# Placing the tiles that DMA writes at multiples of 512 bytes in SBUF, in a two-block cached-attention decode kernel

## The chip, the cores and the metric

The kernel runs on one core of a Trainium2 chip (trn2). The metric is the device time of one execution in microseconds. All runs used here are fast, that is, none was slowed by a lower clock (the granted clock of the tensor engine was 0.72 to 0.74 in every run). In what follows, HBM is the memory that holds the inputs, and SBUF the memory of the core, in 128 partitions, into which DMA (the copying engines) brings them.

## The reference

Two independent attention blocks, A and B, each decode one token for two batch entries; their outputs are concatenated. Cut to what matters:

```python
def _A_ref(x, k_cache, v_cache, wq, wo):      # B is the same
    B, Sq, D = x.shape                        # 2, 1, 640
    Hq, Dh = 32, 192                          # K and V: [2, 32, 8192, 192] bf16
    q = (x @ wq).reshape(B, Sq, Hq, Dh).transpose(0, 2, 1, 3)
    scores = einsum("bhqd,bhkd->bhqk", q, k) * (Dh ** -0.5)
    o = einsum("bhqk,bhkd->bhqd", softmax(scores), v)
    return o.transpose(0, 2, 1, 3).reshape(B, Sq, Hq * Dh) @ wo
```

Each K and V element is used once. The kernel has to bring 837 MB from HBM into SBUF, of which K and V are 805 MB. wq and wo are 15.7 MB each.

## The kernel before

A unit `u` is one (block, head, batch entry); there are 128. The sync engine issues the loads, with two buffers each for K and V. The vector engine multiplies K by q and reduces, the scalar engine sums a quarter of the rows and does the exponentials, the tensor engine multiplies V by the probabilities. What the change and the argument touch:

```python
sb = lambda name, shape, dt: es.enter_context(nc.sbuf_tensor(name, shape, dt))
...
kb = [sb(f"kb{i}", [128, T, Dh], BF16) for i in range(NK)]      # T = 64 rows: 24576 bytes per partition
vb = [sb(f"vb{i}", [128, T, Dh], BF16) for i in range(NV)]
prodA = [sb(f"prodA{i}", [128, NA_MAX, Dh], BF16) for i in range(2)]
# ... cut: the other tiles of the engines
wqs = sb("wqs", [128, 2, DC, HG * Dh], BF16)                    # 1536-byte pieces
wos = sb("wos", [128, HG, 3, D], BF16)                          # four slots of 3840 bytes
# ... cut

def sp_wo(w):
    # ... cut
    src = blocks[blk]["wo"][h0 * Dh:(h0 + HG) * Dh, :].rearrange("(pr p i) n -> p pr (i n)", p=128, i=3)
    return dma(wos[:, (w % 2) * HG // 2:(w % 2 + 1) * HG // 2, :, :].rearrange("p pr i n -> p pr (i n)"), src, wosem)

def sp_k(u, part=None):
    blk, h, b, g = unit(u)
    src = blocks[blk]["k"][b, h].rearrange("(p t) d -> p t d", p=128)
    if part is None:
        return dma(kb[u % NK][:], src, ksem[u % NK])
    # ... cut: the first K load comes in two parts

def sp_v(u, t0=0, t1=None, sm=None):
    # ... cut: the last four V loads come in pieces
        return dma(v_tile(u)[:], src, vsem[u % NV])
```

The kernel's instruction streams are emitted with loops (eight units per turn) on the vector and scalar engine and four on the tensor engine; this matters below for how the experiments are built.

Of the kernel before, what the change touches and what calls it, by code (L numbers as in the profile page):

```python
# [8 lines left out]
BF16 = mybir.dt.bfloat16  # L9
# [93 lines left out]
def build_kernel(nc, blocks, out, cfg=None):  # L103
    cfg = dict(cfg or {})
    NBLK = len(blocks)
    B, Hn, Sk, Dh = blocks[0]["k"].shape
    D = blocks[0]["x"].shape[2]
    assert B == 2 and Dh == 192 and Sk % 256 == 0 and D % 128 == 0
    T = Sk // 128
    DC = D // 128  # L110
# [10 lines left out]
    NK = cfg.get("NK", 2)  # L121
    NV = cfg.get("NV", 2)
    HG = cfg.get("HG", 4)
    if Hn % HG != 0:
        HG = 2
# [20 lines left out]
        return 4 * (qg // 2) + (qg % 2)  # L146

    with ExitStack() as es:
        sb = lambda name, shape, dt: es.enter_context(nc.sbuf_tensor(name, shape, dt))
        ps = lambda name, shape, dt: es.enter_context(nc.psum_tensor(name, shape, dt))  # L150
        sem = lambda name: es.enter_context(nc.semaphore(name))

        kb = [sb(f"kb{i}", [128, T, Dh], BF16) for i in range(NK)]
        vb = [sb(f"vb{i}", [128, T, Dh], BF16) for i in range(NV)]
        prodA = [sb(f"prodA{i}", [128, NA_MAX, Dh], BF16) for i in range(2)]
        prodD = sb("prodD", [128, ND_MAX, Dh], BF16)
        sc = [sb(f"sc{i}", [128, T], F32) for i in range(2)]
# [3 lines left out]
        pb = [sb(f"pb{i}", [128, T // 2, 33], BF16) for i in range(NPB)]  # L161
        rs = [sb(f"rs{i}", [128, 1], F32) for i in range(2)]
        qbc = [sb(f"qbc{i}", [128, 2, Dh], BF16) for i in range(4)]
        wqs = sb("wqs", [128, 2, DC, HG * Dh], BF16)
        wos = sb("wos", [128, HG, 3, D], BF16)
        xT = [[sb(f"xT{k}_{b}", [128, DC], BF16) for b in range(B)] for k in range(NBLK)]
        xbc = [[sb(f"xbc{k}_{b}", [128, DC, 128], BF16) for b in range(B)] for k in range(NBLK)]
        o_sb = sb("o_sb", [33, 2, 2, Dh], F32)
# [290 lines left out]
        for u in range(NU):  # L459
            g = u // B  # L460
# [154 lines left out]
def bass_concat_heads__gqa_block_cached__mha_block_cached__decode_kernel(  # L615
    nc: bass.Bass,
    A_x: bass.AP,
    A_k_cache: bass.AP,
    A_v_cache: bass.AP,
    A_wq: bass.AP,  # L620
    A_wo: bass.AP,
    B_x: bass.AP,
    B_k_cache: bass.AP,
    B_v_cache: bass.AP,
    B_wq: bass.AP,
    B_wo: bass.AP,
    out: bass.AP,
):
    blocks = [
        dict(x=A_x, k=A_k_cache, v=A_v_cache, wq=A_wq, wo=A_wo),  # L630
        dict(x=B_x, k=B_k_cache, v=B_v_cache, wq=B_wq, wo=B_wo),
    ]
    build_kernel(nc, blocks, out)
# [28 lines left out]
```

## Time and profile before

| | before |
|---|---|
| time, median of 4 runs | 1975.26 us (1974.32 to 1975.52) |
| bytes over DMA | 836.79 MB on the load queue |
| busy share: load queue (16 engines) / vector / tensor / scalar | 99.6% / 84% / 56% / 46% |

Lines of the page of the kernel before: busy time of each engine; GB/s in 40 equal slices of the span; packets; the load queue with its packets, MB and share of the 16 DMA engines; and the chain of waits that ended last, by engine.

```profile
PE 1111.1 (56%) x5004; PEld 589.3 (30%) x5004; DVE 1655.7 (84%) x962; ACT 904.1 (46%) x4743; POOL 151.5 (8%) x270
...
GB/s 384 425 429 427 430 426 431 430 425 430 428 430 430 426 431 427 430 430 426 430 426 430 429 427 431 428 427 428 430 431 428 429 428 430 430 426 430 431 429 290
DMA packets 56476, 837.12 MB, mean 424 GB/s; under 512 B 7416, under 2 KB 18304, under 8 KB 23680
...
q1 hardware_dynamic: 56432, 836.79, 99.6%
...
DMA 72%; PE 22%; DVE 5%; issue 1%; SPq 0%; ACT 0%; DVEq 0%
```

The reader should see that nothing but the loads sets the pace: the queue is hardly ever idle (99.6%), its rate is flat from the second slice to the last but one (425 to 431 GB/s), and the chain is mostly loads (72%). The table of windows of the kernel before says the same for three stretches (columns: the stretch and its length, busy time and count of each engine, granted clock, DMA share, GB/s):

```profile
200.00:800.00 600.00, 333.75 (x1507) 177.09 (x1506) 513.67 (x298) 281.71 (x1480) 44.49 (x80) 0.72 1.01 429
800.00:1400.00 600.00, 345.41 (x1546) 182.90 (x1545) 507.84 (x298) 275.88 (x1447) 29.36 (x80) 0.72 1.01 429
1400.00:1900.00 500.00, 284.54 (x1279) 151.12 (x1277) 426.38 (x247) 232.28 (x1219) 23.82 (x65) 0.72 1.01 429
```

Below the page, the trace has one record per DMA packet, with start, duration and size. A packet here is one contiguous row. Here is a digest of the kernel before (durations in ns; smaller pieces of the first and last loads are left out):

```
row (bytes)  what     packets   shortest  median  mean
24576        K, V     32128     912       916     916.7
3840         wo        4096     149       152     152.9
1536         wq        9600      65        68      68.6
```

That is 2008 K/V packets, 256 of wo and 600 of wq for each of the 16 engines, practically without gaps (99.6% of the span). Among the pieces left out are 512 of 12288 bytes; the shortest of them took 460 ns. So two rows of 12288 bytes take at least 920 ns and one of 24576 at least 912: as an estimate from these two, each packet has 8 ns that do not grow with its size (149 and 65 ns, set against 912 in the same way, give 7.7 and 8.5). The records do not name the engine: which packet follows which on one engine is inferred from their ends and starts.

### The profile page before, as it was taken

How to read it: one execution, taken by the hardware profiler on the slowest of the kernel's cores; microseconds unless marked ns; L12 is line 12 of the kernel's file. 1: busy time of each engine (PE TensorE's matmuls, PEld its weight loads, DVE VectorE, ACT ScalarE, POOL GpSimd, SP SyncE). 2: the span in 40 equal slices, each digit the busy share in tenths (PEclk: the TensorE clock that was granted, in tenths of full speed). 3: DMA queues.
4: the chain of work that ended last, by engine and by line, in shares of the span. 5: the costliest groups of instructions: out<-in, count | busy, mean ns of one | idle time of the engine just before them, and what ended most of it. 6: DMA issues, size and time to landing. Idle time of an engine off the chain costs nothing.

```text
span 1973.5 us, 18371 instructions
## 1 busy us (share of the span) xinstructions
PE 1111.1 (56%) x5004; PEld 589.3 (30%) x5004; DVE 1655.7 (84%) x962; ACT 904.1 (46%) x4743; POOL 151.5 (8%) x270
## 2 busy tenths in 40 slices
PE   2546546655655555655655656556555565555657
PEld 1223223322333323322332323223232332223324
DVE  7889898888878888888888888888788887888884
ACT  4445454445445444454444444444445444544442
POOL 4013030000000000000000000000000000000000
PEclk9777777777777777777777777777777776777778
DMA  9999999999999999999999999999999999999996
GB/s 384 425 429 427 430 426 431 430 425 430 428 430 430 426 431 427 430 430 426 430 426 430 429 427 431 428 427 428 430 431 428 429 428 430 430 426 430 431 429 290
DMA packets 56476, 837.12 MB, mean 424 GB/s; under 512 B 7416, under 2 KB 18304, under 8 KB 23680
## 3 DMA queue, kind: packets, MB, share of 16 engines
q1 hardware_dynamic: 56432, 836.79, 99.6%
q8 instruction: 12, 0.20, 0.0%
q14 instruction: 16, 0.13, 0.0%
q10 hardware_dynamic: 16, 0.01, 0.0%
HBM read 836.77 MB, written 0.01 MB: 424 GB/s over the span
## 4 chain that ended last, share of the span: by engine, by line
DMA 72%; PE 22%; DVE 5%; issue 1%; SPq 0%; ACT 0%; DVEq 0%
DMA vb<-in_B_v_cache_dram 36%; DMA vb<-in_A_v_cache_dram 29%; PE ops L402 22%; DMA kb<-in_A_k_cache_dram 7%; DVE prodD L306 3%; DVE prodD L313 1%; DVE prodA L302 0%; DVE sc L317 0%; PE oTps L411 0%; PE oTps L422 0%; PE outps L438 0%; SPq L239 0%; SPq L246 0%; DVE mp L309 0%; ACT oTzL L356 0%
## 5 line engine op out<-in xcount | busy, mean ns | idle before, releaser
L402 PE MATMUL ops<-vb,pb 128*33 128x384 bf16 x4032 | 935.4, 407 | 792.5 <-DMA vb<-in_B_v_cache_dram 398.5
L402 PEld LDWEIGHTS ops<-vb,pb 128*33 128x33 bf16 x4032 | 472.6, 120 | 1246.1 <-DMA vb<-in_B_v_cache_dram 416.6
L324 ACT ACTIVATE prodA<-prodA 128x192 bf16<-128x192 bf16 x2048 | 709.1, 350 | 120.9 <-DVE prodA L302 120.6
L306 DVE TENSOR_TENSOR prodD<-kb,qbc 128x9216 bf16<-128x9216 bf16 x128 | 633.8, 4951 | 3.5 <-DMA kb<-in_A_k_cache_dram 3.5
L313 DVE TENSOR_TENSOR prodD<-prodD 128x4608 bf16<-128x4608 bf16 (+2 forms) x384 | 599.0, 1560 | 13.3
L302 DVE TENSOR_TENSOR prodA<-kb,qbc 128x3072 bf16<-128x3072 bf16 x128 | 225.0, 1757 | 251.1 <-DMA kb<-in_B_k_cache_dram 133.3
L324 ACT ACTIVATION_READ_ACCUMULATOR prodA<-prodA 128x1 f32 x2048 | 386.6, 189 | 0.0
L328 ACT ACTIVATE nb<-mg 128x1 f32<-128x1 f32 x128 | 26.0, 203 | 743.9 <-POOL mg L289 743.9
L289 POOL PARTITION_ALL_REDUCE mg<-mp x128 | 57.7, 451 | 1670.0 <-DVE mp L309 1670.0
L317 DVE TENSOR_REDUCE sc<-prodD 128x48 f32<-128x1152 bf16 x128 | 173.2, 1353 | 4.4
L384 PE MATMUL qps<-wqs,xbc 128*128 (+1 forms) x320 | 67.9, 346 | 51.7 <-ACT qbc L362 40.0
L293 POOL PARTITION_ALL_REDUCE lall<-rs x128 | 83.1, 649 | 114.7 <-ACT pb L331 114.7
L411 PEld LDWEIGHTS oTps<-ones,o_sb 33*128 33x128 f32 x372 | 67.1, 257 | 9.8 <-issue 9.8
L411 PE MATMUL oTps<-ones,o_sb 33*128 33x1 f32 x372 | 69.8, 311 | 0.0
L338 ACT ACTIVATE o_sb<-ops 1x384 f32<-1x384 f32 x63 | 30.0, 476 | 84.0 <-PE oTps L411 71.4
L362 ACT ACTIVATE qbc<-qps 128x384 bf16<-128x384 f32 x64 | 31.3, 488 | 79.1 <-PE qps L384 78.4
L331 ACT ACTIVATE pb<-sc,nb 128x64 bf16<-128x64 f32 x128 | 52.2, 408 | 16.6 <-ACT nb L328 8.3
L384 PEld LDWEIGHTS qps<-wqs,xbc 128*128 128x128 bf16 x320 | 27.1, 101 | 87.0 <-ACT qbc L362 42.2
L309 DVE TENSOR_REDUCE mp<-sc 128x1 f32<-128x64 f32 x128 | 28.2, 220 | 13.4 <-issue 4.4
L438 PE MATMUL outps<-wos,oTz 128*4 (+1 forms) x186 | 31.1, 304 | 14.6 <-ACT oTz L356 14.6
L339 ACT ACTIVATE o_sb<-ops 1x384 f32<-1x384 f32 x63 | 30.3, 481 | 0.7
L331 ACT ACTIVATION_READ_ACCUMULATOR pb<-sc,nb 128x1 f32 x128 | 23.8, 186 | 0.0
(27 smaller groups left out, 78.0 us busy)
## 6 DMA issues: line engine op xcount, KB each, us to landing
vb<-in_A_v_cache_dram SPq DMA_DIRECT2D x64, 3072.0 KB, 22.4
kb<-in_B_k_cache_dram SPq DMA_DIRECT2D x64, 3072.0 KB, 23.2
kb<-in_A_k_cache_dram SPq DMA_DIRECT2D x63, 3072.0 KB, 22.6
vb<-in_B_v_cache_dram SPq DMA_DIRECT2D x60, 3072.0 KB, 22.9
wos<-in_A_wo_dram SPq DMA_DIRECT2D x8, 960.0 KB, 27.2
wqs<-in_B_wq_dram SPq DMA_DIRECT2D x8, 960.0 KB, 24.8
wos<-in_B_wo_dram SPq DMA_DIRECT2D x8, 960.0 KB, 27.2
wqs<-in_A_wq_dram SPq DMA_DIRECT2D x7, 960.0 KB, 24.8
```

The source lines that it names most:

```text
L289: return lambda eng: eng.partition_all_reduce(mg[u % 2][:], mp[u % 2][:], 128, bass.bass_isa.ReduceOp.max)
L293: return lambda eng: eng.partition_all_reduce(lall[g % 2][:, b:b + 1], rs[u % 2][:], 128, bass.bass_isa.ReduceOp.add)
L302: return lambda eng: eng.tensor_tensor(prodA[u % 2][:, 0:na, :], kb[u % NK][:, 0:na, :], qb_bc(u, na), ALU.mult)
L306: return lambda eng: eng.tensor_tensor(prodD[:, 0:T - na, :], kb[u % NK][:, na:T, :], qb_bc(u, T - na), ALU.mult)
L313: return lambda eng: eng.tensor_tensor(prodD[:, 0:nd, 0:w], prodD[:, 0:nd, 0:w], prodD[:, 0:nd, w:2 * w], ALU.add)
L317: return lambda eng: eng.tensor_reduce(sc[u % 2][:, na:T], prodD[:, 0:T - na, 0:24], AXL.X, ALU.add)
L324: return lambda eng: eng.activation(prodA[u % 2][:, t, :], prodA[u % 2][:, t, :], ACTF.Identity, accum_out=sc[u % 2][:, t:t + 1])
L331: return lambda eng: eng.activation(pb[u % NPB][:, :, ::32], sc[u % 2][:].rearrange("p (j a) -> p j a", a=2), ACTF.Exp, bias=nb[u % 2][:], ...
L362: return lambda eng: eng.activation(qbc[qg % 4][:], qps[:, 0:QW].rearrange("p (a d) -> p a d", a=2), ACTF.Identity)
L384: ins = eng.matmul(qps[:, 0:QW], xbc[blk][b][:, c, :], wqs[:, slot, c, off].rearrange("p a n -> p (a n)") if slot is not w % 2 else wqs[:, ...
L402: ins = eng.matmul(ops[(u // B) % 2][0:33, b, 0:QW], pb[u % NPB][:, j, :], vv[:, j, :], start=(j == 0), stop=(j == T // 2 - 1))
L411: ins = eng.matmul(oTps[:, 2 * i + b:2 * i + b + 1], o_sb[:, b, :, :].rearrange("p s (r i) -> p i (s r)", i=3)[:, i, :], ones33[:], start= ...
```

## The change

The intent: every row that DMA writes should start on a 512-byte line of SBUF. Before, the first K tile lies at byte 16512 of a partition, 128 past a multiple of 512, and since the tile sizes are multiples of 512, K, V, wq and the even wo slots all lie at 128 and the odd wo slots at 384. After, all lie at 0. No instruction and no byte is added.

```diff
-        sb = lambda name, shape, dt: es.enter_context(nc.sbuf_tensor(name, shape, dt))
+        sb = lambda name, shape, dt, align=32: es.enter_context(nc.sbuf_tensor(name, shape, dt, align_bytes=align))
...
-        kb = [sb(f"kb{i}", [128, T, Dh], BF16) for i in range(NK)]
-        vb = [sb(f"vb{i}", [128, T, Dh], BF16) for i in range(NV)]
+        LINE = 512
+        WO = 3 * D * 2 // LINE * LINE // 2 + (LINE // 2 if 3 * D * 2 % LINE else 0)
+        kb = [sb(f"kb{i}", [128, T, Dh], BF16, LINE) for i in range(NK)]
+        vb = [sb(f"vb{i}", [128, T, Dh], BF16, LINE) for i in range(NV)]
+        wqs = sb("wqs", [128, 2, DC, HG * Dh], BF16, LINE)
+        wos_p = sb("wos", [128, HG, WO], BF16, LINE)
+        wos = wos_p[:, :, 0:3 * D].rearrange("p g (i n) -> p g i n", i=3)
...
-        wqs = sb("wqs", [128, 2, DC, HG * Dh], BF16)
-        wos = sb("wos", [128, HG, 3, D], BF16)
```

## The prediction

> **What bounds the kernel.** The DMA engines. The page's queue table gives the load queue 99.6% of the 16 engines' span; the table of windows shows a DMA share of 1.00 to 1.01 and 426 to 430 GB/s in every stretch between 50 and 1900 us. The chain of waits is 72% DMA (V loads 65%, K loads 7%). The vector engine is busy 84%, the tensor engine 56%; both wait for loads. Only about 14 us at the start and 12 us at the end (DMA share 0.36 after 1950 us) are something else. So a change helps only as far as it shortens DMA packets.
>
> **What the change does.** It adds and removes no instruction and no byte. K and V rows stay 24576 bytes, wq rows 1536, wo rows 3840. Only SBUF addresses move. In the built program of before, the first K tile lies at 16512, which is 128 past a multiple of 512; K, V and wq sizes are multiples of 512, so K, V, wq and the even wo slots are all at 128 and the odd wo slots at 384. After it, all are at 0. wo is just 15.7 of 836.8 MB; K and V are 805 MB, so K and V decide.
>
> **What it can be worth.** [...] The trace's packet records (32128 such packets) have a minimum of 912, a median of 916, a mean of 916.7[...]. The excess hardly depends on size: minima are 34 ns for 768 bytes[...], 65 for 1536[...], 149 for 3840[...], 460 for 12288[...]. So it is a cost per packet, not a lower rate. Even the 8192-byte instruction-fetch packets have 309[...], and a 4-byte packet takes 9 ns. I therefore take about 8 ns as fixed and independent of the destination's alignment. [...] What could be alignment is in the other 4.7 ns between minimum and mean.
>
> Bounds, as estimates: if every K/V packet fell to its minimum, 2008 packets per engine x 4.7 ns = 9 us. [...] If nothing is alignment, 0. I hold nothing most likely (about 65%), a few us next. wo slots at 128 and 384 give no visible split (149 to 161 ns in one cluster set), and their whole share of packet time is 4096 x 153 ns / 16 = 39 us, 2%[...].
>
> All of a per-packet saving would be on the critical path, since the engines are never idle between 50 and 1900 us.
>
> **Prediction.** 1973 us, 8 in 10 between 1963 and 1978. Faster by over 2%: 0.02; within 2%: 0.97; slower by over 2%: 0.01.
>
> **What would show it.** Packet records after: 24576-byte packets with median 912 to 916; GB/s in the middle stretches 428 to 432; queue share still above 99%; the chain of waits still over 70% DMA; instruction counts 18371 unchanged; busy times of vector and scalar engine within 1%.
>
> **What would make it wrong.** [...] Or engine operands that dislike their new addresses, enough to outlast the DMA: the vector engine has only 16% to spare.

The sum came to 1975 us less nothing (held most likely) to a few us, hence 1973. "Excess" is what a packet takes beyond the part that grows with its size; the "about 8 ns" of it taken as fixed can be had from the shortest times alone, as above: 2 x 460 - 912 = 8 ns.

## More of the kernel before

The scatter between executions of one kernel on one chip is about 0.1% (the kernel before beside runs 1 to 4: 1973.23 to 1975.62 us), so differences of 2 to 3 us out of 1975 can be read when a kernel has several runs. The experiments ran on three chips (1 to 4 and 9 to 12 on one, 5 to 8 and 13 to 16 on a second, 17 and 18 on a third); the kernel before, run beside each group, had medians from 1973.74 to 1975.18 us, so about 1 us of a difference between groups can be the chip.

The vector engine's largest group of the kernel before, from the groups of instructions (line, engine, operation, tiles, count, busy time, mean ns of one, idle time before), for later comparison:

```profile
L306 DVE TENSOR_TENSOR prodD<-kb,qbc 128x9216 bf16<-128x9216 bf16 x128 | 633.8, 4951 | 3.5 <-DMA kb<-in_A_k_cache_dram 3.5
```

## The result

| | before | after |
|---|---|---|
| time, median | 1975.26 us (1974.32 to 1975.52, 4 runs) | 1960.17 us (1960.09 to 1963.61, 4 runs) |
| span of the profiled execution | 1973.5 us | 1961.8 us |

The ratio is 0.9929 (95% interval 0.9912 to 0.9946). A ratio is the mean time of one kernel's fast runs over that of the other's of the same rounds, so it is not quite the ratio of the medians quoted. The kernel is 15 us faster: inside the 2% band as predicted, but 3 us below the lower end of the stated range.

The same lines of the page of the kernel after:

```profile
PE 1115.6 (57%) x5004; PEld 590.1 (30%) x5004; DVE 1656.0 (84%) x962; ACT 903.0 (46%) x4743; POOL 172.8 (9%) x270
...
GB/s 371 429 430 431 432 430 433 431 430 433 431 433 433 429 432 433 431 433 431 432 430 431 432 430 433 431 432 428 435 432 431 432 430 433 431 432 431 432 432 299
DMA packets 56476, 837.12 MB, mean 427 GB/s; under 512 B 7416, under 2 KB 18304, under 8 KB 23680
...
q1 hardware_dynamic: 56432, 836.79, 99.7%
...
DMA 72%; PE 22%; DVE 5%; issue 1%; SPq 0%; ACT 0%; DVEq 0%
```

And the windows of the kernel after:

```profile
200.00:800.00 600.00, 341.84 (x1519) 179.90 (x1518) 517.58 (x302) 281.17 (x1480) 53.85 (x81) 0.72 1.01 432
800.00:1400.00 600.00, 348.48 (x1543) 183.67 (x1542) 511.65 (x296) 281.39 (x1480) 37.34 (x80) 0.73 1.01 432
1400.00:1900.00 500.00, 289.20 (x1293) 154.07 (x1292) 428.44 (x249) 233.35 (x1225) 32.20 (x66) 0.73 1.01 432
```

And the vector engine's group of the kernel after:

```profile
L309 DVE TENSOR_TENSOR prodD<-kb,qbc 128x9216 bf16<-128x9216 bf16 x128 | 633.7, 4951 | 3.6 <-DMA kb<-in_A_k_cache_dram 3.6
```

Packet counts and bytes are the same to the last digit, the vector engine's durations too (4951 ns before and after), the bound is the same. Of what sets the pace only the rate moved, from 429 to 432 GB/s, alike in all three stretches. The packet records say how:

```
row (bytes)  what   shortest   mean before   mean after   95th percentile before -> after
24576        K, V   912        916.7         913.3        921 -> 912
3840         wo     149        152.9         149.1        161 -> 149
1536         wq      65         68.6          65.0         76 ->  65
```

Before, packets were spread above a shortest duration; 83% of the K/V packets took longer than 912 ns (leaving out the few of 1000 ns and more). After, 0.1% did. The shortest duration did not move. Summed per engine, the load queue's packets took 1966.4 us before and 1956.2 after, 10.2 us less; K and V give 2008 x 3.4 ns = 6.8 us, wq 600 x 3.6 = 2.2, wo 256 x 3.8 = 1.0. Packets overlap a little (the DMA share is 1.01), so start to start is the truer cost: the mean for consecutive K/V packets (without the few gaps of 1000 ns and more) fell from 913.4 to 908.9 ns, 4.5 ns or 9.0 us over 2008 packets; wq fell by 3.5 ns and wo by 3.3, 2.9 us more. Together 11.9 us, close to the difference of the two profiled spans (11.7). That it is so close is in part luck: the sum leaves out the packets of 1000 ns and more, which cost 1.2 us per engine before (40 packets) and 2.7 after (296). The unprofiled difference is 15.1; the profiled execution after (1963.61 us) was itself 3.4 us longer than its three companions, and had moved its first 10 MB 1.3 us later than the profiled execution before. Which part of those 3.4 us is what, no trace tells.

### The profile page after: what moved, and what is told of

It reads as the page before. It is cut to its first block, busy times and chain, and to the rows that moved or that the text cites. A ratio compares the mean times of both kernels' runs of the same rounds, so it can differ in the third digit from the quotient of the medians.

```text
span 1961.8 us, 18371 instructions
## 1 busy us (share of the span) xinstructions
PE 1115.6 (57%) x5004; PEld 590.1 (30%) x5004; DVE 1656.0 (84%) x962; ACT 903.0 (46%) x4743; POOL 172.8 (9%) x270
## 3 DMA queue, kind: packets, MB, share of 16 engines
q1 hardware_dynamic: 56432, 836.79, 99.7%
## 4 chain that ended last, share of the span: by engine, by line
DMA 72%; PE 22%; DVE 5%; issue 1%; SPq 0%; ACT 0%; DVEq 0%
DMA vb<-in_B_v_cache_dram 35%; DMA vb<-in_A_v_cache_dram 29%; PE ops L405 22%; DMA kb<-in_A_k_cache_dram 8%; DVE prodD L309 3%; DVE prodD L316 1%; DVE prodA L305 0%; DVE sc L320 0%; PE oTps L414 0%; PE oTps L425 0%; PE outps L441 0%; SPq L242 0%; SPq L249 0%; DVE mp L312 0%; ACT oTzL L359 0%
## 5 line engine op out<-in xcount | busy, mean ns | idle before, releaser
L309 DVE TENSOR_TENSOR prodD<-kb,qbc 128x9216 bf16<-128x9216 bf16 x128 | 633.7, 4951 | 3.6 <-DMA kb<-in_A_k_cache_dram 3.6
L296 POOL PARTITION_ALL_REDUCE lall<-rs x128 | 105.6, 825 | 114.7 <-ACT pb L334 114.7
L441 PE MATMUL outps<-wos,oTz 128*4 (+1 forms) x186 | 31.1, 304 | 15.1 <-ACT oTz L359 15.1
```

What stands on the lines that cost most here:

```text
L296: return lambda eng: eng.partition_all_reduce(lall[g % 2][:, b:b + 1], rs[u % 2][:], 128, bass.bass_isa.ReduceOp.add)
L309: return lambda eng: eng.tensor_tensor(prodD[:, 0:T - na, :], kb[u % NK][:, na:T, :], qb_bc(u, T - na), ALU.mult)
```

## The experiments

One obstacle first. In the looped kernel, waits inside the loops count against a register, which the safety check before a run refuses. All experiments therefore emit the streams written out ("flat"), by dropping the loop argument of three emit calls. Two controls measure what that does.

The theories at the start: **P**, a packet whose destination row starts off a boundary pays a fixed price, whatever its length; rivals **B**, the price is per byte, and **E**, it is the engines' tiles, which moved too, that matter.

In the table, "over shortest" is the share of K/V packets (those under 1000 ns) above 912 ns (in the flat runs about 0.1% or less take less than 912), "mean" their mean duration. "Long" is the summed excess per engine of the packets over 1000 ns. The numbers after "at" are positions modulo 512 bytes.

| run | K, V at | wq, wo at | engine tiles at | median us | over shortest | mean | long, us | wq / wo mean ns |
|---|---|---|---|---|---|---|---|---|
| flat before | 128 | 128 | 128 | 1994.22 | 64% | 915.68 | 11.5 | 67.8 / 152.5 |
| flat after | 0 | 0 | 0 | 1978.67 | 1.5% | 912.40 | 7.2 | 65.3 / 149.2 |
| K, V only aligned | 0 | 128 | 128 | 1979.68 | 2.4% | 912.54 | 8.0 | 65.3 / 149.0 |
| K, V not aligned | 128 | 0 | 0 | 1988.71 | 36% | 914.03 | 10.8 | 65.2 / 149.1 |
| wq, wo only aligned | 128 | 0 | 128 | 1988.26 | 36% | 914.01 | 11.3 | 65.1 / 149.1 |
| K only aligned | 0, 128 | 128 | 128 | 1985.81 | 16% | 913.35 | 10.7 | 66.7 / 150.4 |
| all at 256 | 256 | 256 | 256 | 1977.26 | 1.4% | 912.36 | 7.8 | 65.1 / 149.2 |
| all at 0, no padding | 0 | 0 | 0 | 1978.23 | 1.2% | 912.29 | 6.9 | 65.3 / 149.1 |
| all at 192 | 192 | 192 | 192 | 1994.72 | 77% | 915.80 | 11.2 | 68.0 / 152.9 |
| all at 160 | 160 | 160 | 160 | 1995.06 | 73% | 915.65 | 11.5 | 67.7 / 152.8 |

("Engine tiles at" gives the products and scores; smaller tiles lie where they fall. In "all at 256" the odd wo slots lie at 0, in "all at 0, no padding" at 256.)

### 1 and 2. Controls: the two kernels written out

```diff
-                S_dve.emit(eng, 8)
+                S_dve.emit(eng)
```

and the same for the scalar (8) and tensor engine (4).

> Control: the kernel before, with the three loops of instructions written out (nothing else changed), because waits inside those loops count against a register. All theories: the loads set the pace, so within 0.3% of the kernel before, 1975 us (1971 to 1979); 24576-byte packets mean 916 to 917 ns as before. If it differs by more, all later runs are compared with this one and not with the kernel before.

> Control: the changed kernel with its loops written out. All theories: 15 us under the flat kernel before (12 to 17), 1960 us; 24576-byte packets all at 912 ns, 1536-byte ones all at 65, 3840-byte ones all at 149.

Measured: 1994.22 and 1978.67 us. The expectation that writing out costs nothing was wrong: both are 19 us slower than the looped kernels. The trace shows 39 instruction packets of 16 KB where the looped kernel has 12, and 485 K/V packets of 1000 ns and more where the looped kernel before has 40. But the difference between the two is 15.6 us, and their ratios to the kernel before give 1.0022 / 1.0102 = 0.992: the effect is there in full, and the flat pair is a fair stand-in. From here on runs are compared with the flat pair. Note one difference inside it: of the 15.6 us, about 4 come from the long packets (11.5 against 7.2 us in the table), which cost little in the looped pair, and the other way round (1.2 us before, 2.7 after).

Windows of the flat before, then of the flat after (same columns):

```profile
100.00:600.00 500.00, 272.14 (x1231) 144.22 (x1229) 429.08 (x249) 234.02 (x1231) 55.50 (x67) 0.72 1.01 428
```

```profile
100.00:600.00 500.00, 273.07 (x1235) 145.01 (x1233) 434.48 (x250) 237.72 (x1254) 55.12 (x66) 0.72 1.01 431
```

The same step of 3 GB/s as in the looped pair, with the DMA share at 1.01 in both.

### 3 and 4. Only K and V aligned, and the reverse

```diff
 # K, V only aligned: from the flat before
+        pad0 = sb("pad0", [128, 192], BF16)      # 384 bytes before K
         kb = ...
         vb = ...
+        pad1 = sb("pad1", [128, 64], BF16)       # 128 bytes after V
 # K, V not aligned: from the flat after
-        kb = [sb(f"kb{i}", [128, T, Dh], BF16, LINE) for i in range(NK)]
+        kb = [sb(f"kb{i}", [128, T, Dh], BF16) for i in range(NK)]        # V alike
```

> Only K and V at 0 modulo 512; wq, wo and every engine tile at 128 as before. Theory P (a fixed cost per packet whose row starts off the boundary, whatever its length): K and V keep 6.8 of the 10.2 us of packet time per engine that the change saved, two thirds, so 4 to 6 us over the flat after, about 1965; 1536-byte packets stay at 68 to 69 ns mean. Theory B (a rate per byte; K and V are 96% of the bytes): within 1 us of the flat after. Theory E (it is the engines' operand addresses that matter): no gain, 1975.

> The reverse: wq, wo (padded) and engine tiles at 0 modulo 512 as in the change, K and V at 128 as before. Theory P: a third of the gain, 4 to 6 us under the flat before, about 1970; 1536-byte packets at 65 ns, 24576-byte ones at 916 to 917 mean. Theory B: within 1 us of the flat before. Theory E: the whole gain, 1960.

Measured: 1979.68 and 1988.71 us. No theory got both. Theory E falls with the first run (engine tiles at 128, whole gain but 1 us). Theory P predicted 1965 for it in the looped kernel's terms, 4 to 6 us over the flat after; it was 1 us. Theory B predicted that the second run keeps the whole penalty; it lost 5.5 us.

The packets explain why P failed as stated. In the first run wq and wo rows still lie at 128, yet their packets take 65.3 and 149.0 ns, as in the flat after. In the second, K/V rows at 128 take no more than 912 ns in 64% of the cases. Their share of packets over 912 ns, by 10-us stretch from 230 to 410 us on the trace's clock (which starts 10.7 us before the span), is:

```
start of the stretch, us:  230 240 250 260 270 280 290 300 310 320 330 340 350 360 370 380 390 400
over 912 ns, %:             86  55  85  75  85  85   5   0  10  23  13  61  83  72  85  81  63  87
```

A wq load starts at 290 and a wo load at 322. The fast stretch lies between them, and the same pattern (fast after wq, slow after wo) is there at the next wq loads (412 and 533 us). So a packet off the boundary does not always pay: there are stretches in which it does (55 to 87% over 912 ns) and stretches in which it does not (0 to 23%), and the one changes into the other at these loads. I formed a new theory, **state**: misaligned packets hinder one another only in some phase of the 16 engines to each other.

### 5 to 8. Where the boundary is

Unused bytes in front of K in the flat before shift everything:

```diff
+        pad0 = sb("pad0", [128, 64], BF16)       # 128 bytes; 192, 32 and 16 elements in the others
         kb = [sb(f"kb{i}", [128, T, Dh], BF16) for i in range(NK)]
```

> The flat kernel before with 128 unused bytes in front of K: every tile 128 bytes later, so K, V, wq and the even wo slots at 256 modulo 512, the odd wo slots at 0. Theory 256 (a row must start on a multiple of 256): like the flat after, 1977 to 1980, 24576-byte packets all at 912. Theory 512 (as the change supposes): like the flat before, 1993 to 1996, over half of the packets above 912.

> 384 unused bytes in front: K, V, wq and even wo slots at 0 modulo 512, odd wo slots at 256; order of the tiles as before, no padded slots. Theory 256: like the flat after, 1977 to 1980. Theory 512: within 1 us of the flat after, wo being 2% of the bytes, but 3840-byte packets of the odd slots above 149 where other packets are slow too.

> 64 unused bytes in front: everything at 192 modulo 512 (a multiple of 64, not of 128). Theory that any start off the boundary costs the same: like the flat before, 1993 to 1996. Theory that the cost grows with what is cut off: slower than the flat before by some us.

> 32 unused bytes in front: everything at 160 modulo 512 (a multiple of 32, not of 64). Same cost for any start off the boundary: 1993 to 1996. If a start off 64 bytes costs a part of a write of its own: more than at 192 and at 128, 2000 or over.

Measured: 1977.26, 1978.23, 1994.72, 1995.06 us. Windows of the run at 256, then of the run at 192:

```profile
100.00:600.00 500.00, 274.83 (x1235) 145.37 (x1234) 434.34 (x250) 237.83 (x1254) 55.23 (x66) 0.72 1.01 431
```

```profile
100.00:600.00 500.00, 276.35 (x1235) 145.75 (x1233) 428.65 (x249) 232.63 (x1226) 55.50 (x67) 0.72 1.01 428
```

In these runs the boundary is 256 bytes, not 512, and nothing smaller: at 256 and at 0 the run is as the flat after, with or without padded wo slots; at 128, 160 and 192 it is as the flat before, within 1 us. The smaller misalignments are no dearer than 128. The padding of wo and the move of wq and wo in the change were not needed: 128 unused bytes in front of K do all of it.

### 9 and 10. Twice the packets: per packet or per piece?

K and V loads are issued as two loads of half rows, 12288 bytes each, in the flat before and the flat after:

```diff
-                return dma(kb[u % NK][:], src, ksem[u % NK])
+                return halves(kb[u % NK], src, ksem[u % NK])     # V alike; semaphore counts 32 per tile
+            def fn(eng):
+                eng.dma_start(tile[:, 0:T // 2, :], src[:, 0:T // 2, :]).then_inc(s, 16)
+                return eng.dma_start(tile[:, T // 2:T, :], src[:, T // 2:T, :]).then_inc(s, 16)
```

> The flat kernel before with each K and V load issued as two loads of 12288-byte rows: twice the packets, same bytes, everything at 128 modulo 512. All theories: one more fixed share of about 5 ns per added packet (908.9 ns from start to start for 24576 bytes[...]), 2008 x 5 = 10 us, over the flat before. Theory ends (what a row off the boundary costs arises once per packet, at its ends): the K/V part of the penalty, 9 to 14 us, doubles, so 25 to 30 us over its aligned partner, the run beside it. Theory pieces (it arises at every 256-byte piece of a row): the gap to the aligned partner stays at 15 to 17 us.

> The aligned partner: the flat after with K and V in 12288-byte rows. All theories: about 10 us over the flat after, 1988 (1984 to 1994); 12288-byte packets all at 460 ns.

Measured: 2011.7 and 1988.7 us. The aligned one is 10.0 us over the flat after, as expected: 5.0 ns for each of the 2008 added packets. (912 less the 8 ns estimated above is 904 ns, which gives the same 5 ns as an estimate.) The gap between the two is 23.0 us against 15.6 with whole rows: 7.4 more. That is outside the 15 to 17 of the theory of pieces, and below the 25 to 30 of the theory of ends, whose sizing took the K/V part as 9 to 14 us. The packets settle it: the mean excess of a misaligned K/V packet over its aligned partner is 915.68 - 912.40 = 3.3 ns for 24576 bytes (packets under 1000 ns) and 463.65 - 460.10 = 3.6 ns for 12288 bytes (packets under 520 ns). This part of the price is per packet, not per byte; 2008 added packets per engine x 3.6 ns = 7.2 us, close to the measured growth. The long packets are another part: counting those 88 ns and more over the commonest duration, the misaligned run pays 4.3 us per engine more than its partner with whole rows (11.5 against 7.2) and 5.1 with half rows (12.5 against 7.4). This part did not double, which is why the gap stayed below 25 us.

Windows of the half rows off the boundary, then of those on it:

```profile
100.00:600.00 500.00, 273.83 (x1220) 144.45 (x1218) 425.57 (x246) 231.20 (x1219) 54.93 (x66) 0.71 1.01 424
```

```profile
100.00:600.00 500.00, 270.82 (x1233) 144.04 (x1231) 431.27 (x249) 236.21 (x1243) 55.12 (x67) 0.72 1.01 429
```

424 against 429 GB/s: the step has grown from 3 to 5 GB/s.

### 11 and 12. Only wq and wo aligned; only K aligned

```diff
 # wq, wo only: from "K, V not aligned", the engine tiles back to 128
+        pad1 = sb("pad1", [128, 64], BF16)
         prodA = ...
 # K only: from the flat before
+        pad0 = sb("pad0", [128, 192], BF16)
         kb = ...
+        pad1 = sb("pad1", [128, 64], BF16)
         vb = ...
```

> K, V and engine tiles at 128 modulo 512, only wq and wo (padded) at 0: it asks whether the 5.5 us that the run with K and V off the boundary kept came from wq/wo or from the engine tiles. Theory state (misaligned packets hinder each other only in some phase of the engines to one another, and the aligned wq and wo loads change that phase): 1987 to 1990, with stretches of all-912 packets that begin at a wq load. Theory E (engine tiles): 1993 to 1995, as the flat before but for 1 to 2 us of wq and wo packets.

> K at 0 modulo 512, V and all else at 128. If each K or V packet paid for itself, half of the K/V gain, 1986 to 1988. Theory state (a packet off the boundary pays only while other engines' packets are off it too, and aligned packets in between loosen the engines): clearly less than half of the penalty is left, 1979 to 1984.

Measured: 1988.26 and 1985.81 us. The first equals "K, V not aligned" (1988.71), although its engine tiles are back at 128, and its packets are fast in the same share of cases: the 5.5 us come from wq and wo, and the engine tiles do nothing. By their own packets wq and wo can account for only 600 x 2.7 ns + 256 x 3.4 ns = 2.5 us of it; the rest is K/V packets that became fast though they did not move.

The second run is a miss of the state theory, which expected 1979 to 1984; it fits the plain half of the K/V gain (1986 to 1988) as well or better. Its packets are more telling than its time. In the middle of each load, K packets (on the boundary) take more than 912 ns in 2% of the cases, V packets (off it) in 25%, against 68% and 72% in the flat before. So packets on the boundary do not pay, and packets off it pay much less often when half of the traffic is on it; but the long packets stayed as many (10.7 us), so the time gained only half.

I also looked in the traces of the looped kernel before and of "K, V not aligned" for what a state could be: whether a packet is longer when another engine's packet starts near its own start or end. No distance up to 40 ns stands out (differences under 0.5 ns near its start and under 1 ns near its end). The phase picture in the expectations is thus unsupported; what switches the stretches stays open.

### 13 to 16. Destination alone, or destination against source?

These four give a wrong result. K and V rows are cut to 24320 bytes (95 x 256) and read from byte 0 or 128 of the row in HBM, written to 0 or 128; wq, wo and engine tiles stay at 128. A small memset fills the bytes that no load writes.

```diff
-                return dma(kb[u % NK][:], src, ksem[u % NK])
+                return dma(*cut(kb[u % NK], src), ksem[u % NK])   # V alike
+        OFF, ROW = 64, T * Dh - 128                               # OFF is 0 or 64 elements
+        def cut(tile, src):
+            return (tile[:].rearrange("p t d -> p (t d)")[:, 0:ROW],
+                    src.rearrange("p t d -> p (t d)")[:, OFF:OFF + ROW])
```

> Wrong result on purpose: K and V rows cut to 24320 bytes, source from the row's start, destination at 128 modulo 512, all else as the flat before. 1% fewer bytes, so about 1974 to 1978 (the flat before less 18 us). Both theories: slow, most packets over the shortest time of their size; it is the reference for the next three.

> Wrong result on purpose: the same rows, destination at 0 modulo 512 for K and V (wq, wo and engine tiles at 128). Both theories: 12 to 16 us under the run with source 0 and destination 128, all packets at one time.

> Wrong result on purpose: source from 128 bytes into the row, destination at 128 modulo 512: both off the boundary by the same. Theory D (the destination alone counts): slow, within 3 us of source 0 and destination 128, or slower if the source has a cost of its own. Theory R (the shift between source and destination counts): fast, within 3 us of source 0 and destination 0.

> Wrong result on purpose: source from 128 bytes into the row, destination at 0 modulo 512. Theory D: fast, within 3 us of source 0 and destination 0. Theory R: slow, 12 to 16 us over it. A cost of the source by itself would show here and in the run before this one alike.

Measured (median us, and mean ns of the K/V packets under 1000 ns):

| | destination at 128 | destination at 0 |
|---|---|---|
| source from 0 | 1976.14, 906.33 | 1961.30, 902.75 |
| source from 128 | 1976.36, 906.28 | 1960.46, 902.52 |

Windows with the source from 0, destination at 128, then at 0:

```profile
100.00:600.00 500.00, 275.95 (x1236) 145.60 (x1234) 434.41 (x250) 237.70 (x1254) 58.14 (x66) 0.72 1.01 428
```

```profile
100.00:600.00 500.00, 275.45 (x1254) 146.36 (x1253) 438.71 (x254) 237.80 (x1254) 62.59 (x66) 0.72 1.01 431
```

The destination counts. Moving the source by 128 bytes makes no difference, neither alone nor against the destination. (Where the caches themselves start in HBM is not on record, so this shows what a shift of 128 bytes costs, not that the first source was on a boundary.)

### 17 and 18. Which end of the row?

Wrong again: rows of 24448 bytes (95.5 x 256) have one end off the boundary wherever they start.

```diff
-        OFF, ROW = 0, T * Dh - 128
+        OFF, ROW = 0, T * Dh - 64
```

> Wrong result on purpose: K and V rows cut to 24448 bytes, destination at 0 modulo 512, so each starts on a multiple of 256 and ends 128 bytes past one. By bytes 10 us over the run with source 0, destination 0 and 24320 bytes, which took 1961. If the start decides: 1969 to 1973, all packets at one time. If a cut-off end costs as much: 1983 to 1988. If each end costs half: about 1978.

> Wrong result on purpose: the same rows at 128 modulo 512, so each starts 128 bytes past a multiple of 256 and ends on one. If the start decides: 1984 to 1989, as the run with source 0 and destination 128 plus 10 us. If the end decides: 1969 to 1974. If each end costs half: about 1978.

Measured: 1979.78 with the start on the boundary and the end off it, 1978.03 with the start off and the end on. By bytes alone the run with both ends on it (1961.3) would be 128 x 2008 bytes / 27 bytes per ns = 9.5 us longer, 1970.8 (an estimate; 27 bytes per ns is 24576 bytes in the 908.9 ns from start to start). So one end off costs 9.0 or 7.2 us, and both ends off cost 14.8 (1976.14 - 1961.30). The two runs were on another chip, on which the kernel before took 1 us less (1974.15 against 1975.13), so the two figures can be 1 us too small. Either end costs, by time about half of the two or somewhat more. The packets under 1000 ns agree that either end costs, but put one end nearer to a third: their mean is 2.0 ns over the commonest (907 ns) in both runs, against 4.3 ns over 902 with both ends off and 0.8 with none, so 1.2 of 3.5 ns. The rest of the time of one end lies in the long packets.

Windows with only the end off, then with only the start off; the rate lies between the two of the runs before:

```profile
100.00:600.00 500.00, 278.77 (x1227) 146.56 (x1225) 433.13 (x250) 237.66 (x1253) 56.57 (x66) 0.72 1.01 429
```

```profile
100.00:600.00 500.00, 274.83 (x1228) 144.90 (x1226) 433.19 (x250) 237.95 (x1253) 58.14 (x67) 0.72 1.01 429
```

No version came out of this that beats the changed kernel. The run with 128 bytes of padding alone equals it with a simpler edit, in the flat form; its looped form could not be run.

## Why the prediction was right or wrong

- **The bound: right.** The DMA share stayed at 1.01, the queue's share at 99.7%, the chain at 72% DMA. A saving per packet did come out in full.
- **"I therefore take about 8 ns as fixed and independent of the destination's alignment": right.** The shortest times are the same after as before, 912 ns for 24576 bytes and 460 for 12288, so the 8 ns estimated from them are still there, and 912 is what 99% of the K/V packets fell to.
- **The step that failed: "What could be alignment is in the other 4.7 ns between minimum and mean ... I hold nothing most likely (about 65%)".** The term of alignment in the sum was put at about zero; it measured nearly all of the 4.7 ns. The 4.7 ns was the right place, and its bound ("if every K/V packet fell to its minimum ... 9 us") is what happened: start to start, K/V packets gained 4.5 ns, 9.0 us per engine. Holding zero most likely had no measurement behind it. There was a sign against it in the trace: a narrow shortest time with most packets some ns above it (shortest and median 65 and 68 ns for 1536 bytes, 149 and 152 for 3840, 912 and 916 for 24576) asks for a cause.
- **A term left out.** The sum had K and V only. wq and wo gained 3.5 and 3.3 ns per packet, 2.9 us together. They are 4% of the bytes but a quarter of the sum, because the price is for the most part per packet (3.3 ns at 24576 bytes, 3.6 at 12288) and their rows are short. What caused it is another matter: in the flat form, aligning K and V alone already brought the wq and wo packets down to 65.3 and 149.0 ns and the run to within 1 us of the whole gain, so "K and V decide" held. The range's lower end of 1963 left 12 us for everything; 11.9 us is what the two traces show, and 15.1 what the unprofiled runs show, so even the corrected sum is 3 us short of the median, and no trace tells why.
- **An argument that could not have worked.** I read "wo slots at 128 and 384 give no visible split" as a sign against alignment. Both are off the 256-byte boundary, so no split was to be expected.
- What the runs show is a boundary of 256 bytes in the destination, at both ends of a row: 1977.26 us with all at 256 against 1994.72 at 192, and 1979.78 with the end alone off it against 1970.8 with both ends on it, the estimate of runs 17 and 18. Nor is the cost the number of bytes past the boundary: it was no greater at 192 (1994.72) than at 128 (1994.22).

What is shown: 256 bytes (1977.26 us with all at 256, 1994.72 at 192), in the destination (1961.30 at 0, 1976.14 at 128), at either end of the row (9.0 and 7.2 us), for the most part per packet (3.3 ns at 24576 bytes, 3.6 at 12288), and not the engine tiles (1988.26 with them at 128, 1988.71 at 0). What is not shown: the mechanism in the memory or the DMA engine, why there are more long packets off the boundary, and why a packet off the boundary pays in some stretches and not in others. The packets do act on one another: with K on the boundary and V left at 128, V packets above 912 ns fell from 72% to 25%. How they do so stays open.

## What to carry to other kernels

In a kernel that is bound by DMA all the time, look at the distribution of packet durations of one size: if most lie a few ns above a sharp shortest time, print the addresses of the destination tiles modulo 256. Let both ends of each row in SBUF fall on multiples of 256 bytes (here 128 unused bytes before the first tile suffice); it added no instruction here, and the gain was some 4 ns per packet: 0.7% in all with rows of 24 KB, and, as an estimate from 3.5 ns on 65, about 5% of the time of loads whose rows are 1.5 KB, a kernel that no run here tested.
